# Reordering the routing tail of a mixture-of-experts kernel: the last group's gates and one-hot ahead of the lead's norms, free first weights, more constants, norms ahead of transposes

## The chip, the core and the metric

The kernel runs on one core of one Trainium2 chip. The metric is the device time of one execution in microseconds. The core has a matrix engine (PE, with its weight loads as PEld), a vector engine (DVE), an activation engine (ACT), GpSimd (POOL) and a queue engine (SP) that issues most DMAs. The engines run side by side and wait for each other through semaphores.

## The reference

```python
kv = np.einsum('bhsd,bhse->bhde', k, v)            # 8 batches, 8 heads, 576 tokens, 64 wide
out = np.einsum('bhsd,bhde->bhse', q, kv)
rms = np.sqrt(np.mean(out * out, axis=-1, keepdims=True) + 1e-06)
x = (out / rms * g_norm)                           # then 4608 rows of 512
...
logits = x @ w_gate
e_idx = np.argmax(logits, axis=1)                  # one expert of 8 for each row
probs = np.exp(logits - logits.max(-1, keepdims=True))
probs /= probs.sum(-1, keepdims=True) + 1e-09
eom = 1.0 / (1.0 + np.exp(-(x @ w_output_gate)))
for e in range(E):
    h = np.maximum(x[mask] @ w1[e], 0.0)           # 512 -> 1024
    out[mask] = gate_w[mask, None] * eom[mask, e, None] * (h @ w2[e])
```

## The kernel before, in words

The 4608 rows are 36 tiles of 128. A first stage makes kv for each batch, then the attention rows of each tile (`out_tile`, L779), their squares (L795, summed on DVE at L805) and the gate products. Rows go to a scratch tensor `xs` in DRAM, because the second stage reads them sorted by expert.

**Routing.** The tiles form three groups of 16, 10 and 10 (`GR`). `route(gi)` is a generator of ten steps: 1 the norms (L826 to L842), 2 the gate products scaled by them (`gp`, L850), 3 the logits' sum, maximum and one-hot (`lg` to `ohb`, L854 to L873), 4 the ranks' matmuls (`mrp<-erow`, `ohsum`, `ohb`, L886 to L893) and the output gate (L899 to L902), 5 two exponentials on ACT (L905, L906), 6 slots and scales (L909 to L926) and the rows' write to `xs` (`xwrite`, L980), 7 the row patterns `rrl` and `la` (L933 to L940, `la` partly on POOL), 8 ten or sixteen small matmuls and the lead expert's index (L943 to L952), 9 the patterns `rrc` for all experts (L956 to L959), 10 their matmuls (L962).

**The lead.** The expert with most rows among the first 16 tiles is known early. Its first 256 rows are the lead: `gather(0)` (L250, an indirect DMA on POOL from `xs`) fetches two tiles `xg`; `stage(0, k)` scales each by its norms on DVE (`scale_heads`, L268), copies a column (`tl`, L287), transposes on PE (`tps`, L291) and copies to `xT` on ACT (L294). Eight `lead1` (L320, `hps`) are the first weight product, sixteen matmuls at L567 (`yps`) the second.

**The second run.** The rest of the same expert's rows, 436, come with `gather(1)` in four tiles. `stage(1, k)` stands behind the lead's last matmuls f = 4 to 7 of L567: norms on DVE (L268), `tl`, four transposes on PE, a copy to `xT` on ACT (L299) and its remainder on DVE (L300). Its first product (`mm1`, L341) needs all four tiles. Runs 2 to 8, one expert each, follow on PE.

**What sets the order.** On PE, ACT, DVE and POOL the instructions stand as the program writes them. SP's order is set by a scheduler. After the last tile the string `TAIL` gives the order by hand: `Q` finishes the rows, a digit advances that group's `route`, `W` loads the lead's second weights, `C` issues eight matmuls on constants (L687, `kvp<-ones`) whose result nobody reads, `L` is the next step of the lead (two stages, eight `lead1`), `g` is `gather(1)`, `K` ranks the other experts.

**DMA order.** Rows of the first 16 tiles are written once all inputs are loaded; then the lead's four first-weight loads (`wraw`, 512 KB each, L197) are issued, with `behind` making them wait for a row write, and then the rows of group 1:

```python
for c in range(4):
    behind(wload(0, 1, c), written[0 if c > 1 else -1])
open_rows(1)
```

DMAs on SP use eight semaphores in turn (DMAHW0 to DMAHW7); a DMA waits until the one before it on the same semaphore has landed.

Of the kernel before, what the change touches and what calls it, by code (L numbers as in the profile page):

```python
# [42 lines left out]
TMAX = 6  # L43
# [11 lines left out]
RUNS = [(0, 0, LEAD), (0, LEAD // P, CAP[0] - LEAD)] + [(p, 0, CAP[p]) for p in range(1, E)]  # L55
# [16 lines left out]
PLACES = ['P', 'P', 'VVP']  # L72

HOOKS = {34: "G"}
TAIL = "Q1W2CCCCCCLL122LL22L22LL2gL00L11L22K"

COLD = (24, (8, 8, 10, 5), 5, 4, 12, 8)

# [45 lines left out]
def tiles_of(i):  # L124

    _, t0, n = RUNS[i]
    return [(t0 + k, k * P, min(P, n - k * P)) for k in range(-(-n // P))]
# [6 lines left out]
def body(ctx: ExitStack, tc: tile.TileContext, kvm, rem, qT, wg, gn, w1, w2, kc, xs, tab, out):  # L134
    nc = tc.nc
# [35 lines left out]
    def take(shape, dt, name):  # L171

        i = (rfree if name == "xrow" else free).pop(0)
        t = mem.tile(shape, dt, name=name, tag=f"slot{i}")
        held[id(t)] = (i, t)
        return t

    def give(t):
        i, t = held.pop(id(t))
        (rfree if loads and i >= SLOTS - ROWS else free).append(i)  # L180
# [3 lines left out]
    def expert(p, eng):  # L184
        e = ET.Pool if eng is nc.gpsimd else ET.SP
        k = (p, eng is nc.gpsimd)
        if k not in ereg:
            ereg[k] = nc.values_load(epos[0:1, p:p + 1], engines=(e,), min_val=0, max_val=E - 1)
        return ereg[k]
# [3 lines left out]
    def wload(p, which, c, eng=None):  # L193
        r = take([P, 1024], F32, "wraw")
        eng = eng or nc.sync
        src = (w1 if which == 1 else w2)[ds(expert(p, eng), 1), c]
        d = eng.dma_start(out=r, in_=src.rearrange("o p x -> p (o x)"))  # L197
        raw[(p, which, c)] = r
        return d
# [35 lines left out]
    xg, tails, xT, hT = {}, {}, {}, {}  # L235
# [3 lines left out]
    def behind(a, b):  # L239

        tc.add_manual_dep(a.ins, b.ins.name,
                          mybir.DependencyInfo(mybir.DependencyClass.Sync, mybir.DependencyReason.DATA),
                          reason="place in time")
# [21 lines left out]
    def scale_heads(x, eng):  # L265
        v = x[:, 0:DM].rearrange("p (h d) -> p h d", d=D)
        f = x[:, C_RMS:C_RMS + H].unsqueeze(2).to_broadcast([x.shape[0], H, D])
        return eng.tensor_tensor(out=v, in0=v, in1=f, op=ALU.mult)  # L268

    def scale_rows(i, k0=0, k1=TMAX, after=None):  # L270
        for k, (t, c0, M) in list(enumerate(tiles_of(i)))[k0:k1]:
            scaled = scale_heads(xg[(RUNS[i][0], t)][:M], nc.gpsimd)
            if after is not None:
                behind(scaled, latest[after])

    def stage(i, k):
        p = RUNS[i][0]
        t, c0, M = tiles_of(i)[k]
        x = xg.pop((p, t))
        scale_heads(x[:M], nc.vector)  # L280
        if k == 0:
            if i == 0:
                xT[i] = take([P, 4, LEAD], F32, "xT")
            else:
                xT[i] = [[mem.tile([P, 4, CMAX], F32R, name="xT", tag=f"xT{j}")] for j in range(2)]
        tl = cst.tile([P, 1], F32, name="tl", bufs=14)
        nc.vector.tensor_copy(tl[:M], x[:M, C_SCALE:C_SCALE + 1])  # L287
        tails[(p, t)] = tl
        ps = ps_b.tile([P, 2, 512], F32, name="tps", tag="big")[:, 0].rearrange("p (c m) -> p c m", c=4)
        for c in range(4):  # L290
            nc.tensor.transpose(ps[:, c, :M], x[:M, c * P:(c + 1) * P], ident[:M, :M])  # L291
        give(x)
        if i == 0:
            nc.scalar.activation(xT[0][:, :, c0:c0 + M], ps[:, :, :M], AF.Copy, scale=gcol[:, 0:1])  # L294
            return
        for j, (hi, lo) in enumerate(zip(*xT[i])):
            n = hi.shape[1]
            v = ps[:, j * n:(j + 1) * n, :M]
            nc.scalar.copy(hi[:, :, c0:c0 + M], v)  # L299
            nc.vector.tensor_tensor(out=lo[:, :, c0:c0 + M], in0=v,  # L300
                                    in1=hi.bitcast(F32)[:, :, c0:c0 + M], op=ALU.subtract)
# [357 lines left out]
    for i in range(2):  # L659
        o = c1.tile([P, GMAX + 1, E], BF16, name=f"ohb{i}")  # L660
# [82 lines left out]
    while g < NT:  # L743
        if g == 0:
            k = NT - sum(BIG.values()) - 2 * ROWS
            x = c1.tile([P, k, XW], F32, name="xrow0")
        elif g in BIG:
            k = BIG[g]
            x = mem.tile([P, k, XW], F32, name="xrow", tag=f"xT{list(BIG).index(g)}")
        else:  # L750
            k = 2
            x = take([P, k, XW], F32, "xrow")
# [5 lines left out]
    def out_tile(g):  # L758
        gi, t, n = group_of(g)
        if t == 0:  # L760
            gst[gi] = (sm.tile([P, GMAX, E], F32, name="ss"),
                       sm.tile([P, max(GR[gi % 2::2]), 16, H], F32, name=f"gp{gi % 2}", bufs=1),
                       sm.tile([P, GMAX, 16], F32, name="lg"))
        ps = ps_b.tile([P, 2, 512], F32, name="ops", tag="big")
        parts = []
        n0 = g * P
        while n0 < (g + 1) * P:
            b = n0 // S
            n1 = min((g + 1) * P, (b + 1) * S)
            parts.append((b, n0 - g * P, n1 - n0))  # L770
            n0 = n1
        v = ps[:, :, 0:NP * W].rearrange("q u (p y) -> q u p y", p=NP)
        for p in range(NP):
            for b, r0, m in parts:
                q0 = g % 2 * P + r0

                for u in range(2):
                    r = slice(u * D, (u + 1) * D)
                    nc.tensor.matmul(v[r0:r0 + m, u, p, :], qt[g // 2][r, p, q0:q0 + m], augs[b % 3][r, p, :],  # L779
                                     start=True, stop=True)  # L780
        if g % 2:
            give(qt.pop(g // 2))
        outs.append((g, ps))

    def out_rows():

        g, ps = outs.pop(0)
        gi, t, n = group_of(g)
        ss, gp, lg = gst[gi]
        c0, k, x = next(c for c in chunks if c[0] <= g < c[0] + c[1])  # L790
        xrow = x[:, g - c0]
        v = ps[:, :, 0:NP * W].rearrange("q u (p y) -> q u p y", p=NP)
        nc.scalar.copy(xrow[:, 0:DM].rearrange("q (p u d) -> q u p d", p=NP, u=2), v[:, :, :, 0:D])
        sq = wk.tile([P, H, D], F32, name="sq", bufs=3)
        nc.scalar.activation(sq.rearrange("q (u p) d -> q u p d", u=2), v[:, :, :, 0:D], AF.Square)  # L795
        nc.scalar.copy(gp[:, t].rearrange("q x (u p) -> q u p x", u=2), v[:, :, :, D:W])
        squares.append((sq, ss[:, t, :], gi if t + 1 == n else None))
# [169 lines left out]
            vec.tensor_tensor(out=tsum, in0=tps, in1=tsum, op=ALU.add)  # L967

    xwrites = []
    written = []  # L970
    lead_known = []

    opened = [False, False]
# [1 line left out]
    def xwrite(g, o, i):  # L975
        late = g >= LEAD_TILES
        if not opened[late]:
            xwrites.append((g, o, i))
            return
        written.append(nc.sync.dma_start(out=o, in_=i))  # L980
        if id(i) in held:
            give(i)

# [14 lines left out]
    def steps(at):  # L998
        for gi in list(routing):
            for _ in range(STEPS[gi].get(at, 0)):  # L1000
                advance(gi)

    def run_out(limit):
        nonlocal done_tiles
        if done_tiles < limit:
            out_tile(done_tiles)
            done_tiles += 1
            if len(outs) > 1:
                out_rows()
            if len(squares) > 1:  # L1010
                sums()
            steps(done_tiles)
            load()
            if not loads and not opened[0]:
                open_rows(0)
            if lead_known and opened[0] and not opened[1]:
                for c in range(4):
                    behind(wload(0, 1, c), written[0 if c > 1 else -1])
                open_rows(1)
            for step in HOOKS.get(done_tiles, ""):  # L1020
                act(step)
# [25 lines left out]
    def p1_main():  # L1047
# [16 lines left out]
        while done_tiles < NT:  # L1064
            run_out(NT)
        for step in TAIL:
            act(step)
# [134 lines left out]
    with fixed:  # L1202
# [12 lines left out]
        for i in range(len(RUNS)):  # L1215
# [57 lines left out]
            def put(k, f, e, *a):  # L1273
                at.setdefault(k, {}).setdefault(f, []).append(lambda: e(*a))
# [4 lines left out]
            end = order[T - 1]  # L1279
            if i == 0:  # L1280
                for k in range(len(tiles_of(1))):
                    put(end, 4 + k, stage, 1, k)
            if i > 1:
                put(order[0], 0, begin, i, 1)
# [4 lines left out]
            if change:  # L1289
# [11 lines left out]
                for j in range(2):  # L1301
                    k = 3 + j + (i == 1)
# [20 lines left out]
    with ExitStack() as p3:  # L1323
# [4 lines left out]
        with tc.For_i(0, nreg) as i:  # L1328
# [19 lines left out]
            for w in (w1, w2):  # L1348
                for c in range(4):
                    t = wo.tile([P, 1024], F32, name=f"ow{len(ws)}")  # L1350
                    nc.sync.dma_start(out=t, in_=w[ds(eo, 1), c].rearrange("o p x -> p (o x)"))
                    ws.append(t)
            x = so.tile([P, XW], F32, name="ox")
# [9 lines left out]
            for f in range(8):  # L1363
                ph = pt.tile([P, P], F32, name="oph")
                for d in range(4):
                    o = d * 256 + (f % 2) * P
# [3 lines left out]
            for f in range(8):  # L1370
# [5 lines left out]
                                         in_=y, in_offset=None, bounds_check=NTOK - 1, oob_is_err=False)  # L1376
# [49 lines left out]
```

## Time and profile before

| what | value |
|---|---|
| median of three runs | 567.3 us (566.47 to 567.6) |
| the profiled execution's own time | 567.28 us |
| its span in the trace | 565.4 us |
| PE busy, weight loads | 538.2 us (95%), 460.1 us (81%) |
| DVE, ACT, POOL busy | 386.5 us (68%), 295.1 us (52%), 265.8 us (47%) |
| DMA | 92.28 MB, mean 163 GB/s |
| mean granted clock of PE | 0.985 |

The span runs from the first to the last instruction; 1.9 us of the execution lie around it. PE is nearly always busy, so the stretches in which it is not, or in which its clock is granted at half, carry most of what can be changed by order alone.

### The profile page before, as it was taken

To read this page: it belongs to the slowest core of one execution; us is meant where nothing else is said; L and a number is where in the kernel's file an instruction comes from. 1 tells how busy PE (TensorE), PEld (TensorE's weight loads), DVE (VectorE), ACT (ScalarE), POOL (GpSimd) and SP (SyncE) were. 2 spreads that over 40 slices of the span, in tenths; PEclk is the share of its full clock that TensorE was granted. 3 is DMA by queue.
4 is the path that set the end of the run, shared out by engine and by line. 5 is a ranking of instruction groups with operands and counts; after the bars stand their busy time and mean duration, and the time that the engine had idled before them with its cause. 6 is when DMAs were issued, how large, how long until landed. Compare 5 with 4: busy or idle time off the path is not lost.

```text
span 565.4 us, 11013 instructions
## 1 busy us (share of the span) xinstructions
PE 538.2 (95%) x4104; PEld 460.1 (81%) x4104; DVE 386.5 (68%) x820; ACT 295.1 (52%) x604; POOL 265.8 (47%) x295
## 2 busy tenths in 40 slices
PE   9999994997999999999999999999999999999995
PEld 6888883853978997889889878987898789779974
DVE  2236994673579978847994898577757978896700
ACT  1577881222456746545564456555554656475510
POOL 3001255131498168414970595079408943991021
PEclk9999997799999999999999999999999999999998
DMA  7999998851403360425125513450525054215001
GB/s 302 417 416 416 415 368 308 330 191 56 168 24 112 134 204 22 152 92 174 69 86 172 160 61 112 147 197 20 187 70 192 35 188 129 107 51 175 2 23 44
DMA packets 28424, 92.28 MB, mean 163 GB/s; under 512 B 3825, under 2 KB 3825, under 8 KB 28368
## 3 DMA queue, kind: packets, MB, share of 16 engines
q1 hardware_dynamic: 21936, 71.63, 34.7%
q0 software_dynamic: 6432, 19.92, 10.3%
q8 instruction: 34, 0.56, 0.4%
q14 instruction: 22, 0.18, 0.1%
HBM read 72.34 MB, written 19.70 MB: 163 GB/s over the span
## 4 chain that ended last, share of the span: by engine, by line
PE 62%; DVE 14%; DMA 7%; issue 6%; POOL 5%; ACT 4%; SPq 1%; POOLq 0%; ACTq 0%; DVEq 0%
PE yps L586 25%; PE hpsa L474 13%; PE hpsd L474 6%; PE hps L474 4%; DMA xg<-xs,gidx 3%; PE yps L580 3%; PE hps L320 3%; DVE hT L497 3%; DVE ss L805 2%; PE ops L779 2%; DMA ld<-qT 2%; DMA ld<-kvm 2%; POOL xg L268 2%; PE kvp L704 2%; ACT hT L494 2%
## 5 line engine op out<-in xcount | busy, mean ns | idle before, releaser
L586 PE MATMUL yps<-whi,hT 128*128 128x512 f32 (+3 forms) x560 | 185.0, 396 | 0.5 <-DVE hT L497 0.4
L586 PEld LDWEIGHTS yps<-whi,hT 128*128 128x128 f32 (+3 forms) x560 | 103.9, 186 | 24.1 <-DVE hT L497 1.3
L586 PE MATMUL yps<-wlo,hT 128*128 128x512 f32 (+3 forms) x280 | 109.9, 392 | 0.0
L600 POOL DMA_INDIRECT out<-y,oidx x42 | 51.0, 1213 | 124.9 <-ACT y L599 79.2
L250 POOL DMA_INDIRECT xg<-xs,gidx x42 | 44.9, 1070 | 88.4 <-ACT hT L494 28.1
L497 DVE SCALAR_TENSOR_TENSOR hT<-ct,hT 128x256 fp32r<-128x256 f32 (+6 forms) x88 | 52.2, 623 | 22.6 <-ACT hT L494 22.6
L586 PEld LDWEIGHTS yps<-wlo,hT 128*128 128x128 f32 (+3 forms) x280 | 52.1, 186 | 9.9
L494 ACT ACTIVATE hT<-ct 128x328 fp32r<-128x328 f32 (+13 forms) x56 | 34.4, 614 | 43.0 <-DVE ct L508 43.0
L474 PE MATMUL hpsd<-xT,wh 128*128 128x328 f32 (+6 forms) x224 | 48.3, 302 | 1.7 <-DVE ct L541 1.7
L474 PE MATMUL hpsa<-xb,wh 128*128 128x328 f32 (+6 forms) x224 | 48.2, 303 | 1.1 <-ACT sn L540 0.7
L474 PE MATMUL hpsa<-xT,wh 128*128 128x328 f32 (+6 forms) x224 | 47.5, 300 | 0.0
L268 POOL TENSOR_TENSOR xg<-xg 128x512 f32<-128x512 f32 (+7 forms) x36 | 42.3, 1184 | 9.8 <-DVE ct L529 9.5
L805 DVE TENSOR_REDUCE ss<-sq 128x8 f32<-128x512 f32 x36 | 23.8, 680 | 30.1 <-ACT sq L795 30.1
L399 DVE SCALAR_TENSOR_TENSOR wl<-wraw,gcol,wh 128x512 fp32r<-128x512 f32 (+1 forms) x56 | 43.8, 821 | 0.2 <-ACT wh L398 0.2
L227 DVE TENSOR_TENSOR wlo<-wraw,whi 128x1024 fp32r<-128x1024 f32 x32 | 39.9, 1247 | 5.7 <-ACT whi L224 5.5
L599 ACT ACTIVATE y<-yps,tl 128x512 f32<-128x512 f32 (+3 forms) x37 | 25.5, 689 | 33.3 <-PE yps L586 19.2
L474 PEld LDWEIGHTS hpsd<-xT,wh 128*128 128x128 f32 x224 | 36.6, 188 | 5.1 <-DVE ct L541 3.9
L474 PEld LDWEIGHTS hpsa<-xb,wh 128*128 128x128 f32 x224 | 36.6, 188 | 4.9 <-ACT sn L540 4.2
L399 DVE SCALAR_TENSOR_TENSOR wl<-ws,gcol,wh 128x1024 fp32r<-128x1024 f32 x28 | 40.0, 1429 | 0.0
L779 PE MATMUL ops<-aug,ld 64*128 64x80 f32 (+1 forms) x640 | 39.3, 271 | 0.3 <-issue 0.2
L474 PEld LDWEIGHTS hpsa<-xT,wh 128*128 128x128 f32 x224 | 37.0, 188 | 1.7 <-ACT sn L532 0.3
L779 PEld LDWEIGHTS ops<-aug,ld 64*128 64x128 f32 (+1 forms) x640 | 33.8, 176 | 3.6 <-issue 1.6
(233 smaller groups left out, 1156.8 us busy)
## 6 DMA issues: line engine op xcount, KB each, us to landing
wraw<-w SPq DMA_DIRECT2D x64, 512.0 KB, 4.4
ld<-kvm SPq DMA_DIRECT2D x32, 512.0 KB, 9.9
ld<-qT SPq DMA_DIRECT2D x18, 512.0 KB, 10.0
xs<-xrow SPq DMA_DIRECT2D x9, 528.0 KB, 11.4
xs<-xrow SPq DMA_DIRECT2D x2, 1320.0 KB, 7.4
xs<-xrow SPq DMA_DIRECT2D x1, 2112.0 KB, 12.4
ld<-rem SPq DMA_DIRECT2D x4, 512.0 KB, 9.9
xg<-xs,gidx POOLq DMA_INDIRECT x42, 4.0
```

The costliest lines, as they stand in the source:

```text
L227: eng.tensor_tensor(out=lo, in0=r, in1=hi.bitcast(F32), op=ALU.subtract)
L250: gathered = nc.gpsimd.indirect_dma_start(out=x[:M, :], out_offset=None, in_=rows, in_offset=bass.IndirectOffsetOnAxis(ap=gidx[:M, p, t:t ...
L268: return eng.tensor_tensor(out=v, in0=v, in1=f, op=ALU.mult)
L399: nc.vector.scalar_tensor_tensor(out=lo, in0=x, scalar=gcol[:, 0:1], in1=hi.bitcast(F32), op0=ALU.mult, op1=ALU.subtract)
L474: nc.tensor.matmul(ps, W[a][d], X[b][d], start=start and k == 0, stop=k == 5, skip_group_check=not start)
L494: S.activation(hh, x, AF.Relu)
L497: V.scalar_tensor_tensor(out=v(o, j1 - j0), in0=x[..., j0:j1], scalar=0.0, in1=hh[..., j0:j1].bitcast(F32), op0=ALU.max, op1=ALU.subtract)
L586: nc.tensor.matmul(ps[:M], a, b, start=(f == 0 and j == 0), stop=(f == 7 and j == 2))
L599: nc.scalar.activation(y[:M], ps[:M], AF.Copy, scale=tl[:M, 0:1])
L600: i_ = nc.gpsimd.indirect_dma_start(out=out, out_offset=bass.IndirectOffsetOnAxis(ap=oidx[:M, p, t:t + 1], axis=0), in_=y[:M], in_offset=N ...
L779: nc.tensor.matmul(v[r0:r0 + m, u, p, :], qt[g // 2][r, p, q0:q0 + m], augs[b % 3][r, p, :], start=True, stop=True)
L805: nc.vector.tensor_reduce(out=o, in_=sq, axis=AX.X, op=ALU.add)
```

## The change

```diff
-TAIL = "Q1W2CCCCCCLL122LL22L22LL2gL00L11L22K"
+TAIL = "Q1W2CCCCCCCCCCC22LL22LL22LL12gLL00L11L22K"
...
-    def scale_rows(i, k0=0, k1=TMAX, after=None):
+    def scale_rows(i, k0=0, k1=TMAX, after=None, eng=nc.gpsimd):
         for k, (t, c0, M) in list(enumerate(tiles_of(i)))[k0:k1]:
-            scaled = scale_heads(xg[(RUNS[i][0], t)][:M], nc.gpsimd)
+            scaled = scale_heads(xg[(RUNS[i][0], t)][:M], eng)
...
         x = xg.pop((p, t))
-        scale_heads(x[:M], nc.vector)
+        if i == 0:
+            scale_heads(x[:M], nc.vector)
...
-    written = []
...
-        written.append(nc.sync.dma_start(out=o, in_=i))
+        nc.sync.dma_start(out=o, in_=i)
...
                 for c in range(4):
-                    behind(wload(0, 1, c), written[0 if c > 1 else -1])
+                    wload(0, 1, c)
                 open_rows(1)
...
             if i == 0:
                 for k in range(len(tiles_of(1))):
+                    put(end, k, scale_rows, 1, k, k + 1, None, nc.vector)
                     put(end, 4 + k, stage, 1, k)
```

The string has 11 `C` for 6, so 88 constant matmuls for 48. Group 2's steps 2 and 3 stand ahead of the lead's two stages, its steps 4 and 5 ahead of the first `lead1`, its steps 6 and 7 ahead of the third; step 8 of groups 1 and 2 and `gather(1)` stand behind the fourth, and two `lead1` instead of one stand between `gather(1)` and group 0's step 9.

DVE behind group 2's norms (`rv` in the row above these): `xg` and `tl` are the lead's two stages, `tsl` is group 1's step 8, the others group 2's steps 2 to 4. Before:

```order
L268 TENSOR_TENSOR xg<-xg 128x512
L287 COPY tl<-xg 128x1
L268 TENSOR_TENSOR xg<-xg 128x512
L287 COPY tl<-xg 128x1
L947 TENSOR_TENSOR tsl<-mrp,tsl 128x12
L850 TENSOR_TENSOR gp_1195<-gp_1195,rv 128x10x64 x2
L854 TENSOR_REDUCE lg<-gp_1195 128x10x8
L861 TENSOR_REDUCE mx<-lg 128x10
```

After:

```order
L851 TENSOR_TENSOR gp_1195<-gp_1195,rv 128x10x64 x2
L855 TENSOR_REDUCE lg<-gp_1195 128x10x8
L862 TENSOR_REDUCE mx<-lg 128x10
L864 TENSOR_TENSOR rd<-lg,mx 128x80
L867 SCALAR_TENSOR_TENSOR rsc<-rd,cf 128x80
L869 TENSOR_REDUCE rsx<-rsc 128x10
L873 MEMSET ohb_121 128x4
L874 TENSOR_TENSOR ohb_121<-rsc,rsx 128x80
L268 TENSOR_TENSOR xg<-xg 128x512
L288 COPY tl<-xg 128x1
L268 TENSOR_TENSOR xg<-xg 128x512
L288 COPY tl<-xg 128x1
```

The gates and the one-hot moved ahead of the lead's norms, and `tsl` moved far behind them.

SP behind the last of the five lead row writes; `xs<-xrow` are group 1's row writes, `wraw<-w` the lead's first weights, and the brackets name what each waits for. Before:

```order
L980 DMA xs<-xrow 128x2x528 [waits DVE_49,DMAHW3_49,Activation_49,Pool_49]
L197 ISA
L197 DMA wraw<-w 128x1024 [waits DMAHW4_49,DMAHW2_49,PE_49]
L197 ISA
L197 DMA wraw<-w 128x1024 [waits DMAHW5_49,PE_49]
L197 ISA
L197 DMA wraw<-w 128x1024 [waits DMAHW6_49,PE_49]
L197 ISA
L197 DMA wraw<-w 128x1024 [waits DMAHW7_49,PE_49]
L980 DMA xs<-xrow 128x2x528 [waits DVE_49,DMAHW0_49,Activation_49,Pool_49]
```

After:

```order
L197 DMA wraw<-w 128x1024 [waits DMAHW3_49,PE_49]
L197 ISA
L197 DMA wraw<-w 128x1024 [waits DMAHW4_49,PE_49]
L197 ISA
L197 DMA wraw<-w 128x1024 [waits DMAHW5_49,PE_49]
L197 ISA
L197 DMA wraw<-w 128x1024 [waits DMAHW6_49,PE_49]
L980 DMA xs<-xrow 128x2x528 [waits DVE_49,DMAHW7_49,Activation_49,Pool_49]
L980 DMA xs<-xrow 128x2x528 [waits DVE_49,DMAHW0_49,Activation_49,Pool_49]
```

The weights stand ahead of all of group 1's row writes now, and the wait for the last lead row write (DMAHW2) is gone from the first of them; DMAHW6 of the fourth is the first lead row write.

DVE at the second run, behind the split of two weights; `xg` are the norms, `xT` the remainders. Before:

```order
L268 TENSOR_TENSOR xg<-xg 128x512
L287 COPY tl<-xg 128x1
L300 TENSOR_TENSOR xT<-tps,xT 128x4x128
L268 TENSOR_TENSOR xg<-xg 128x512
L287 COPY tl<-xg 128x1
L300 TENSOR_TENSOR xT<-tps,xT 128x4x128
```

After:

```order
L268 TENSOR_TENSOR xg<-xg 128x512 x3
L268 TENSOR_TENSOR xg<-xg 52x512
L288 COPY tl<-xg 128x1
L301 TENSOR_TENSOR xT<-tps,xT 128x4x128
L288 COPY tl<-xg 128x1
L301 TENSOR_TENSOR xT<-tps,xT 128x4x128
```

All four norms stand ahead of the first remainder now.

## Rows read from the trace of the kernel before

**Rows 1.** The page's first part: busy us, share, instructions.
```profile
PE 538.2 (95%) x4104; PEld 460.1 (81%) x4104; DVE 386.5 (68%) x820; ACT 295.1 (52%) x604; POOL 265.8 (47%) x295
```

**Rows 2.** Windows of 2.5 us: length, busy of PE, PEld, DVE, ACT, POOL, granted clock, DMA share, GB/s.
```profile
90.00:92.50 2.50, 0.00 (x0) 0.00 (x0) 0.11 (x1) 0.00 (x0) 2.46 (x5) 0.78 0.96 361
...
102.50:105.00 2.50, 2.50 (x8) 1.96 (x7) 2.08 (x8) 0.38 (x1) 0.00 (x0) 0.50 1.04 392
105.00:107.50 2.50, 2.50 (x24) 2.17 (x23) 0.79 (x5) 0.64 (x3) 0.00 (x0) 0.99 0.77 313
```

**Rows 3.** PE in order of time: start, length, instruction, count, idle before it.
```profile
83.73 5.08 PE L687 MATMUL kvp<-ones 128*128 128x256 bf16 x45
96.63 1.08 PE L291 MATMUL tps<-ident,xg 128*128 128x128 f32 x4 [7.82 <-DVE tl L287]
98.15 1.08 PE L291 MATMUL tps<-ident,xg 128*128 128x128 f32 x4 [0.43 <-DVE tl L287]
...
100.01 6.20 PE L320 MATMUL hps<-xT,wraw 128*128 128x256 f32 x16 [0.53 <-ACT xT L294]
106.05 0.20 PE L886 MATMUL mrp<-erow,row 128*128 128x88 bf16 x1
...
106.44 5.41 PE L320 MATMUL hps<-xT,wraw 128*128 128x256 f32 x24
...
114.67 0.84 PE L962 MATMUL mrp<-rrc,la 128*128 128x96 bf16 x16 [0.74 <-DVE rrc L959]
...
119.99 11.39 PE L567 MATMUL yps<-wraw,hT 128*128 128x512 f32 x26
131.22 0.60 PE L291 MATMUL tps<-ident,xg 128*128 128x128 f32 x4
131.65 1.02 PE L567 MATMUL yps<-wraw,hT 128*128 128x512 f32 x2
133.92 0.66 PE L291 MATMUL tps<-ident,xg 128*128 128x128 f32 x4 [1.24 <-DVE tl L287]
...
139.26 0.42 PE L291 MATMUL tps<-ident,xg 52*128 52x52 f32 x4 [1.18 <-issue]
140.10 0.88 PE L341 MATMUL hps<-xT,whi 128*128 128x436 f32 x2 [0.42 <-ACT xT L299]
```

**Rows 4.** DVE in order of time.
```profile
89.87 0.24 DVE L840 SCALAR_TENSOR_TENSOR rv<-ru,ry 128x80 f32<-128x80 f32 x1
95.68 0.69 DVE L268 TENSOR_TENSOR xg<-xg 128x512 f32<-128x512 f32 x1 [5.57 <-DMA xg<-xs,gidx]
...
97.20 0.69 DVE L268 TENSOR_TENSOR xg<-xg 128x512 f32<-128x512 f32 x1 [0.77 <-DMA xg<-xs,gidx]
...
99.61 1.55 DVE L850 TENSOR_TENSOR gp<-gp,rv 128x640 f32<-128x640 f32 x2
...
103.18 0.81 DVE L854 TENSOR_REDUCE lg<-gp 128x80 f32<-128x640 f32 x1
...
126.56 0.68 DVE L268 TENSOR_TENSOR xg<-xg 128x512 f32<-128x512 f32 x1
```

**Rows 5.** SP's DMA issues in order of time.
```profile
86.88 2.13 SPq L197 DMA_DIRECT2D wraw<-w  x4
```

**Rows 6.** POOL's gathers in order of time.
```profile
89.21 0.96 POOL L250 DMA_INDIRECT xg<-xs,gidx  x1 [0.30 <-DVE ry L837]
...
118.59 1.04 POOL L250 DMA_INDIRECT xg<-xs,gidx  x1 [8.97 <-DVE tsum L967]
```

**Rows 7.** DMA issues of 89.0 to 89.5, median us from issue to landing.
```profile
xg<-xs,gidx POOLq DMA_INDIRECT x1, 8.0
```

**Rows 8.** The same of 118.4 to 119.0.
```profile
xg<-xs,gidx POOLq DMA_INDIRECT x1, 3.5
```

**Rows 9.** Two windows, columns as in rows 2.
```profile
83.00:87.00 4.00, 4.00 (x43) 3.56 (x40) 3.90 (x19) 2.67 (x7) 0.00 (x0) 1.00 0.42 151
...
87.00:88.00 1.00, 1.00 (x12) 0.89 (x10) 0.90 (x6) 0.00 (x0) 0.18 (x1) 1.00 1.03 389
```

## The prediction

> **What bounds the kernel now.** The page's first part comes first: PE is busy for 95% of the span [rows 1], so only the stretches where it is idle, or granted half its clock, have time to give. The windows of 2.5 us show where that is: PE does nothing from 90 to 92.5, its granted clock is 0.78 there on average, 0.50 still from 102.5 to 105, and 0.99 from 105 on [rows 2]. The order of time on PE gives the waits one by one [rows 3]. The constants begin at 83.73 and last 5.08 us, to 88.8. Then PE waits 7.82 us for the lead's first scaled tile. It transposes two tiles, waits 0.53 for their copy, and starts the lead's first product at 100.01 at half clock. At 114.67 it waits 0.74 for group 0's patterns. Between the lead's last matmuls and the second run's four transposes stand three waits of 1.24 (shown), a like one, and 1.18 us. The order of time on DVE tells who is late [rows 4]. The lead's two norms wait for the gather (until 95.68 and 97.20), while DVE has been idle since `rv` at 90.1; group 2's gates begin only behind them, at 99.61. At the second run each norm stands behind the remainder of the tile before it, so each transpose waits for a copy on ACT, a remainder and a norm, although the first norm of the four runs at 126.56, 4.7 us ahead of its transpose.
>
> From 140.10 on PE has other work in every window, and what follows is started by PE's progress. So I count what the change does to the start of the second run's first product, 140.10 [rows 3], and let the rest shift by as much.
>
> **The change, part by part.**
>
> *Norms ahead of transposes.* All four norms run in a row from 126.56, at 0.68 us each: done by 129.3, ahead of the first transpose at 131.22 [rows 3, 4]. The three waits go: 1.24 + 1.18 + one between them, taken as their mean of 1.21, makes 3.6 us. A pair on L567 that is followed by a wait takes 1.02 us; the 13 pairs in a row take 11.39 / 13 = 0.88 [rows 3]. Three of those save 0.14 each, 0.4. What is late next is ACT's copy of the last tile (0.42, already there), and that stays. Sum **-4.0 us**. The cover is the 1.9 us between 129.3 and 131.22; if DVE came that much later the first transpose would wait. The rest of the change moves DVE and PE ahead together, and the second gather is moved ahead by more: its rows are written some 7 us earlier, because group 2's ranks, at 106.05 before, come right behind the lead's transposes, at about 98.6. Bounds: 0 (the norms are late all the same) and -4.4 (the last wait gone as well).
>
> *Gates and one-hot ahead of the norms.* From `rv` at 90.1 the two products (1.55) and the sum to one-hot take until 93.7, as they took from 99.61 to 103.18 before [rows 4]. That fits ahead of the gather at 95.68: they cost nothing while the gather lands after 93.7, and if it landed at its earliest, 92.7 (below), up to 1.0. The ranks' matmuls (106.05 to 106.44, 0.39) then fall into the 0.53 us in which PE waits for ACT's copy: -0.39. Group 1's ten small matmuls, which ran in that gap, now stand between two `lead1`: at most the same 0.39 back. With two `lead1` instead of one behind the indices, group 0's patterns have twice the time, and the 0.74 us wait at 114.67 goes. Sum **-0.7 us**. Bounds: -1.1 and 0.
>
> *First weights not held back.* The four loads were issued from 86.88, when the last lead row write had landed [rows 5]. Now nothing holds the first three, and the fourth waits only for the first lead row write. They follow the lead's rows in SP's queue and fill engines that run empty from 83 to 87: there the DMA share is 0.42, against 1.03 from 87 to 88 at 389 GB/s [rows 9]. That hole takes (1 - 0.42) x 4 us x 389 GB/s = 0.9 MB of the 2.1 MB. On the other hand group 1's five row writes (528 KB each) are no longer behind the weights' wait. Before, one was issued ahead of the weights and four behind; now all five can be sent as soon as their scales are ready, ahead of the gathers. So the gathers have less of the weights beside them and more rows. The second gather was issued at 89.21 and took 8.0 us beside the weights; with nothing beside it a gather took 3.5 [rows 6 to 8]. So it lands between 92.7 and, if it has to wait for everything in front of it, some 100.4: ahead of it stand 1.2 MB of weights and 2.7 MB of rows instead of 2.1 MB and 0.54 MB, 1.26 MB more, at 389 GB/s 3.2 us. I take 7.0 us, near the loaded end, since the queue is still full: landing at 96.2 instead of 97.2, **-1.0 us**.
>
> The Trainium skill (DMA: Bandwidth & Descriptors, Queues, rings and completion order) says that each DMA engine takes turns between queues, a packet at a time, so a gather on POOL's queue would not stand behind what SP has queued. By that the rows in front cost little and the sum would be nearer the early end. The 8.0 us beside SP's loads [rows 7] is more than turn-taking alone seems to ask for, so the trace agrees with it in part at most.
>
> *More constants.* 40 more at 5.08 / 45 to 5.12 / 48, about 0.107 us, are 4.3 us: PE is busy until 93.1 instead of 88.8. Nothing waits for PE before the first tile's transposes, some 0.95 us behind its gather (96.63 - 95.68), so at 95 or so they cost nothing; with the gather at its earliest, 0.8 at most. What they can bring is the clock. It fell from 1.00 in the window of 90 to 92.5, within 3.7 us of the last constant, and came back about 105, after 5 us of unbroken products [rows 2, 3]. What half clock costs: the first 16 recorded matmuls of `lead1` took 6.20, at full clock 24 take 5.41, so 16 take 3.6; and the second tile's transposes took 1.08 against 0.60 to 0.66. Together 2.6 + 0.4 = 3.0 us. With the constants ending at 93.1, PE still has only two groups of transposes (at most 1.08 each) and 0.39 us of ranks until the product begins at about 98.6 to 99.0: some 5.5 us with 1.3 to 2.5 us of work. Before, the clock fell within 3.7 us of silence. I take it that it falls again and comes back after as long: **0**. Bounds: 0 and -3.0.
>
> *Sum.* -4.0 - 0.7 - 1.0 = -5.7 us, against the profiled execution's 567.28, which is the median (567.3) within 0.02: **561.5 us**. What the second run's later stages need (the second gather, the other experts' ranks, the weight loads behind them) starts earlier by the same or more, so nothing there should give it back.
>
> **The rivals.**
>
> *The clock holds.* The first idle stretch is now about 2 us instead of 7.82, and from 132 to 140 three waits of more than 1 us each between transposes did not lower it [rows 2, 3]. Against it: most of the 5.5 us is idle. Then 3.0 more: 558.5.
>
> *The gather is served in turns.* With the weights out of its way it takes 3.5 to 5 us and lands at 92.7 to 94.2, 3 to 4.5 ahead; less 1.0 for gates and constants that are in its way then, 2.0 to 3.5. That gives 558.5 to 560, and as the idle stretch shrinks with it, the clock may hold too: about 557. For it speaks the hole in the transfers [rows 9], against it the five row writes.
>
> *The gather is served in order.* The row writes in front of it cost the 3.2 us above, and it lands at 100.4: 567.28 + 3.2 - 4.7 = 565.8. For it: 8.0 us beside 2.6 MB is about what that data needs.
>
> *The norms are ahead to no avail.* DVE or the second gather comes too late, and the four transposes wait as before: 561.5 + 4.0 = 565.5. Against it the 1.9 us of cover.
>
> *Slower.* The weights do not use the hole, because the engines that are empty are not those with the long queues, and the gather stands behind all of them, the five row writes and a first load of the second weights: 2.1 + 2.7 + 0.5 MB and the gathers' own 0.54 are 5.86 MB, at 389 GB/s 15.1 us from 87, and 2.8 for a landing (3.5 less its own transfer). It lands at 104.9, 7.7 late, PE idles through it at half clock, and the time is 567.28 + 7.7 - 4.7 = 570.3. It decides from 4.7 us on (landing at 101.9) and is a slowdown beyond 0.2%, 1.13 us, from 103.0. Against it: loads issued 10 us before the gather.
>
> **How the numbers follow.** 0.2% is 1.1 us, about what a measurement of this kernel can tell from no change. The forecast, with the gather some 2 us to either side (559.5 to 563.5), has 0.50; the clock holds 0.23; turns 0.08; in order 0.09; norms to no avail 0.03; a gather so late that it cancels the gain 0.03; slower 0.04. The first five are faster: 0.93. Same 0.03, slower 0.04. The range leaves out the upper rivals and half of the turns, 0.2 or a little more: 557.0 to 564.6.
>
> **What the changed profile would show.** Right: no wait over 0.2 us on PE between the transposes of the second run, whose `mm1` starts 4.7 to 4.9 us after the first of them instead of 8.9; DVE's `gp` from 90.1; no wait ahead of group 0's L962 matmuls; weights issued by SP before 82; the second lead norm at 95 to 98; a clock that dips between 94 and 106. Wrong: a second lead norm beyond 99 or before 94, a clock of 1.00 throughout, or a new wait behind 140 that takes back what came before.

## The result, and the profile after

| what | before | changed |
|---|---|---|
| median, runs of one session | 566.88 us (566.15 to 567.6, 4 runs) | 560.26 us (559.43 to 561.48, 4 runs) |
| the profiled execution's own time, span | 567.28, 565.4 us | 559.43, 557.6 us |
| mean granted clock of PE | 0.985 | 0.994 |

The ratio is 0.9885, with a 95% interval of 0.9861 to 0.9909: the changed kernel is about 6.6 us faster, where 5.8 (561.5 against 567.3) was forecast. The profiled execution was the shortest of the four, so sizes read from it lie on the high side. Line numbers of the changed kernel are one higher than those of before from L288 to the matmuls at L963, and the same again at L980; in e5 and e7 they are one higher still.

PE in order of time, with start, length, instruction, count and the idle time before it, answers to [rows 3]:

```profile
83.22 9.78 PE L688 MATMUL kvp<-ones 128*128 128x256 bf16 x88
95.07 0.63 PE L292 MATMUL tps<-ident,xg 128*128 128x128 f32 x4 [2.07 <-DVE tl L288]
96.67 0.81 PE L292 MATMUL tps<-ident,xg 128*128 128x128 f32 x4 [0.97 <-ACT xT L295]
...
98.25 8.22 PE L321 MATMUL hps<-xT,wraw 128*128 128x256 f32 x32 [0.15 <-ACT xT L295]
106.30 0.40 PE L944 MATMUL mrp<-rrl,la 128*128 128x12 bf16 x10
106.96 0.39 PE L944 MATMUL mrp<-rrl,la 128*128 128x12 bf16 x10 [0.26 <-DVE tsl L948]
107.21 3.70 PE L321 MATMUL hps<-xT,wraw 128*128 128x256 f32 x16
110.75 0.84 PE L963 MATMUL mrp<-rrc,la 128*128 128x96 bf16 x16
...
116.08 11.39 PE L568 MATMUL yps<-wraw,hT 128*128 128x512 f32 x26
127.30 0.60 PE L292 MATMUL tps<-ident,xg 128*128 128x128 f32 x4
...
132.16 0.88 PE L342 MATMUL hps<-xT,whi 128*128 128x436 f32 x2 [0.42 <-ACT xT L300]
```

The constants now take 9.78 us; before, the whole of them began at 83.39 and took 5.41 (48 matmuls), since the first row of [rows 3] starts inside them. The second run's first product begins at 132.16, before at 140.10 [rows 3]: 7.94 us sooner, and the execution is 7.85 us shorter, so nothing behind that point gave the gain back. The 7.94 can be split at three instructions that both traces have.

- From the first transpose of the second run to that product: 4.86 us (127.30 to 132.16) instead of 8.88. That is **-4.02**; the three waits are gone, and only ACT's copy of 0.42 is left. (The third wait of before, which the prediction took as 1.21, was 1.14.)
- To the second lead norm, by DVE's rows below: 95.72 instead of 97.20, **-1.48**. From there to the lead's product 2.53 instead of 2.81, **-0.28**; the second tile's transposes take 0.81 instead of 1.08, because the clock falls later.
- From the lead's product (98.25) to the second product (116.08): 17.83 instead of 19.98, **-2.15**. The wait of 0.74 at L963 is gone. The ranks' 0.39 left this stretch, and group 1's small matmuls came in with 0.65 (106.30 to 107.21 holds both groups' ten, 0.91, where before one group's ten took 0.26, from 111.69 to 111.95). That makes -0.48; what remains, -1.67, is in the main the product running less at half clock.

DVE in order of time, for [rows 4]:

```profile
89.98 0.27 DVE L841 SCALAR_TENSOR_TENSOR rv<-ru,ry 128x80 f32<-128x80 f32 x1
90.35 1.73 DVE L851 TENSOR_TENSOR gp<-gp,rv 128x640 f32<-128x640 f32 x2
...
93.97 0.24 DVE L874 TENSOR_TENSOR ohb<-rsc,rsx 128x80 bf16<-128x80 f32 x1
94.13 0.68 DVE L268 TENSOR_TENSOR xg<-xg 128x512 f32<-128x512 f32 x1
...
95.72 0.69 DVE L268 TENSOR_TENSOR xg<-xg 128x512 f32<-128x512 f32 x1 [0.85 <-DMA xg<-xs,gidx]
...
122.97 2.48 DVE L268 TENSOR_TENSOR xg<-xg 128x512 f32<-128x512 f32 x4
```

Group 2's gates and one-hot fill the time from 90.35 to 94.1. The first lead norm stands right behind them, without a wait; the second waits 0.85 for its gather, at 95.72. POOL issued the two gathers at 87.37 and 88.77:

```profile
87.37 1.09 POOL L250 DMA_INDIRECT xg<-xs,gidx  x1 [9.23 <-DVE rrl L934]
88.77 0.96 POOL L250 DMA_INDIRECT xg<-xs,gidx  x1 [0.30 <-issue]
```

The four norms of the second run end at 125.4, 1.9 us ahead of the transposes at 127.30: the cover that the prediction counted.

Windows of the changed kernel, columns as in [rows 2] and [rows 9]:

```profile
83.00:87.00 4.00, 4.00 (x41) 3.52 (x40) 3.90 (x19) 2.67 (x7) 0.00 (x0) 1.00 1.03 405
...
95.00:97.50 2.50, 1.46 (x12) 1.22 (x13) 1.72 (x4) 0.69 (x1) 2.50 (x5) 0.90 1.05 395
97.50:100.00 2.50, 2.35 (x17) 1.93 (x15) 2.14 (x15) 0.94 (x3) 0.99 (x4) 0.50 1.03 416
100.00:102.50 2.50, 2.50 (x12) 2.15 (x12) 1.71 (x9) 0.38 (x1) 1.11 (x2) 0.92 1.02 403
```

The hole in the transfers from 83 to 87 is filled: DMA share 1.03 where it was 0.42 [rows 9]. The clock is at half in the whole window of 97.5 to 100 and in parts of the two beside it, from about 97.0 to 100.4 by windows of 0.5 us; before it was at half until 105 [rows 2].

SP's issues, for [rows 5]:

```profile
77.48 3.73 SPq L197 DMA_DIRECT2D wraw<-w  x4
85.70 4.24 SPq L980 DMA_DIRECT2D xs<-xrow  x5
```

The four weight loads start at 77.48 instead of 86.88. Group 1's five row writes now go out from 85.70 to 89.9, around the two gathers.

### The profile page after: what moved, and what is told of

Its sections match the earlier page's. It is cut to its first block, busy times and chain, and to the rows that moved or that the text cites. A ratio compares the mean times of both kernels' runs of the same rounds, so it can differ in the third digit from the quotient of the medians.

```text
span 557.6 us, 11092 instructions
## 1 busy us (share of the span) xinstructions
PE 539.2 (97%) x4144; PEld 462.6 (83%) x4144; DVE 387.0 (69%) x820; ACT 295.1 (53%) x604; POOL 268.0 (48%) x295
## 4 chain that ended last, share of the span: by engine, by line
PE 69%; POOL 7%; DMA 7%; DVE 6%; issue 6%; ACT 4%; SPq 1%; POOLq 0%; ACTq 0%
PE yps L587 26%; PE hpsa L475 13%; PE hpsd L475 6%; PE ops L780 5%; PE hps L475 4%; PE kvp L705 3%; PE yps L581 3%; PE hps L321 3%; PE yps L568 2%; DVE hT L498 2%; DMA ld<-qT 2%; DMA ld<-kvm 2%; POOL xg L250 2%; POOL xg L268 2%; DMA wraw<-w 1%
## 5 line engine op out<-in xcount | busy, mean ns | idle before, releaser
L601 POOL DMA_INDIRECT out<-y,oidx x42 | 52.2, 1242 | 122.3 <-ACT y L600 81.9
```

Of the source, the lines that this page charges most:

```text
L601: i_ = nc.gpsimd.indirect_dma_start(out=out, out_offset=bass.IndirectOffsetOnAxis(ap=oidx[:M, p, t:t + 1], axis=0), in_=y[:M], in_offset=N ...
```

## The experiments

Two sessions, four kernels each; the kernel before ran beside them with medians of 566.80 (11 runs) and 567.11 us (11 runs). Ratios compare each kernel with the one before in its own session.

**The changed kernel again (e0).** No edit.

> The changed kernel once more, as the measure for the runs beside it. If the clock's fall between the constants and the lead's first product is what spreads its times, they spread again over some 2 us around 560.3 (559.4 to 561.5), and this profile shows the fall at another place than 97.0 to 100.4, with the second run's first product later by about half of any further time at half clock.

Measured: 560.71 us (560.29 to 562.08, 4 runs), ratio 0.9889 [0.9874, 0.9903]. The profile fell on the longest of the four runs:

```profile
97.42 1.08 PE L292 MATMUL tps<-ident,xg 128*128 128x128 f32 x4 [1.30 <-DVE xg L268]
...
99.28 9.48 PE L321 MATMUL hps<-xT,wraw 128*128 128x256 f32 x32 [0.15 <-ACT xT L295]
...
129.89 0.60 PE L292 MATMUL tps<-ident,xg 128*128 128x128 f32 x4
...
134.75 0.88 PE L342 MATMUL hps<-xT,whi 128*128 128x436 f32 x2 [0.42 <-ACT xT L300]
```

The same program takes 9.48 us for the first 32 recorded matmuls of the lead's first product, where the first profile had 8.22, and its second norm stands at 96.47 instead of 95.72. The norms' part is the same 4.86 us. The clock falls at nearly the same place as in the first profile, about 97.2, and not at another as expected, but it comes back only at about 104.0 instead of 100.4. So one program differs from run to run by some 2 us, through the length of the stretch at half clock and the landing of one gather.

**The norms alone (e1).** The kernel before, with this part of the change only:

```diff
+                    put(end, k, scale_rows, 1, k, k + 1, None, nc.vector)
                     put(end, 4 + k, stage, 1, k)
...
-        scale_heads(x[:M], nc.vector)
+        if i == 0:
+            scale_heads(x[:M], nc.vector)
```

> The kernel before with one part of the change: the second run's four norms ahead of its transposes. Theory (three waits of 1.2 us on PE go, and nothing later takes it back): 4.0 us faster than before, 566.9 to 562.9, the first product 4.9 us behind the first transpose instead of 8.9. Rival (DVE or the gather is late all the same, or a later stage waits instead): no change or less than 2 us.

Measured: 563.25 us (562.60 to 563.68, 5 runs), ratio 0.9933 [0.9920, 0.9946], 3.8 us of 567. Its transposes and the product behind them:

```profile
131.15 0.60 PE L292 MATMUL tps<-ident,xg 128*128 128x128 f32 x4
...
136.01 0.88 PE L342 MATMUL hps<-xT,whi 128*128 128x436 f32 x2 [0.42 <-ACT xT L300]
```

They are again 4.86 us apart, and all that stands ahead of them is as before (the second product at 119.93, before 119.99). This part is worth its nearly 4 us by itself, and leaves some 2.5 for the rest.

**The first weights held back (e2).** The changed kernel, with the old wait put back:

```diff
-                    wload(0, 1, c)
+                    behind(wload(0, 1, c), written[0 if c > 1 else -1])
```

> The changed kernel with the first weights held behind the row writes again. Theory (the weights beside the gather are what makes it slow): the second lead tile is scaled at about 97.2 instead of 95.7, and with a longer idle stretch behind the constants the clock is low for longer: 1.5 to 3 us slower than the changed kernel, 561.8 to 563.3. Rival (group 1's rows, which now stand in front of the gather, slow it as much as the weights did): landing at 95.7 or earlier, 560.3 or less.

Measured: 562.01 us (560.08 to 564.18, 6 runs), ratio 0.9918 [0.9899, 0.9938], against 0.9889 for the change. The weights are issued at 85.91 again, but the second norm starts between the two profiles of the changed kernel (95.72 and 96.47):

```profile
95.94 0.69 DVE L268 TENSOR_TENSOR xg<-xg 128x512 f32<-128x512 f32 x1 [0.66 <-DMA xg<-xs,gidx]
```

So the time is in the theory's range, but the profile does not show the later landing (97.2) that was to cause it; the medians differ by 1.3 us with overlapping intervals. Whether the free weights bring something by themselves stays open.

**Six constants (e3).** The changed kernel with the old number of `C`:

```diff
-TAIL = "Q1W2CCCCCCCCCCC22LL22LL22LL12gLL00L11L22K"
+TAIL = "Q1W2CCCCCC22LL22LL22LL12gLL00L11L22K"
```

> The changed kernel with six groups of constants instead of eleven. Theory (the constants shorten the time at half clock and do nothing else): the gather lands as in the changed kernel, the clock falls before the first transposes and rises later, so the lead's first matmuls run longer at half clock: 1 to 2.6 us slower, 561.3 to 562.9. Rival (the clock falls and rises the same way whatever the constants do): 560.3, and the low stretch as long as with eleven.

Measured: 560.97 us (560.86 to 562.71, 5 runs), ratio 0.9903 [0.9889, 0.9917]: 0.3 us more than the changed kernel by medians, 0.8 by ratios, inside the intervals. Three of its windows show why so little:

```profile
92.50:95.00 2.50, 0.00 (x0) 0.00 (x0) 1.15 (x6) 0.00 (x0) 2.50 (x5) 0.50 1.03 397
...
100.00:102.50 2.50, 2.50 (x8) 2.11 (x9) 2.36 (x17) 0.04 (x1) 1.62 (x3) 0.69 0.87 349
102.50:105.00 2.50, 2.50 (x13) 2.21 (x12) 0.82 (x5) 0.77 (x2) 0.20 (x1) 1.00 1.01 381
```

The clock is at half earlier, in the whole window of 92.5 to 95, but PE does nothing there; the product's first 32 matmuls, from 99.83, take 8.02 us, no more than the 8.22 and 9.48 with eleven. By windows of 0.5 us the clock is low from about 91.3 to 101.6; with eleven groups it fell at 97.0 and 97.2 and came back at 100.4 and 104.0. So constants that end before the next work put the fall off, but no gain of theirs shows in the product or in the time. Neither expectation came out: the low stretch is longer, as the theory had it, but the product is not.

**One more constant in the gap (e4).** The changed kernel with 13 `C`, and one `C` between the lead's two stages:

```diff
-TAIL = "Q1W2CCCCCCCCCCC22LL22LL22LL12gLL00L11L22K"
+TAIL = "Q1W2CCCCCCCCCCCCC22LCL22LL22LL12gLL00L11L22K"
```

> The changed kernel with 13 groups of constants ahead of the gates and one more between the lead's two transposes, so that PE idles for 1.5 us and less at a time. Theory (what is left of the clock's cost is set by idle time between the constants and the product): the clock stays at 1.00 through the tail, the product runs at full rate from its first matmul, 1.3 to 2.8 us faster than the changed kernel, 558 to 559.4. Rival (the clock falls at whatever idle stretch there is, and the constants only delay the transposes): 560.3 or slower, with the clock at half for 3 us or more.

Measured: 559.41 us (558.56 to 559.79, 4 runs), ratio 0.9869 [0.9854, 0.9883]. All windows from 90 to 105 have a granted clock of 1.00, and so have those up to 117; the lead's first product runs at full clock throughout:

```profile
94.86 0.63 PE L292 MATMUL tps<-ident,xg 128*128 128x128 f32 x4 [0.29 <-DVE tl L288]
95.32 1.04 PE L688 MATMUL kvp<-ones 128*128 128x256 bf16 x8
97.36 0.63 PE L292 MATMUL tps<-ident,xg 128*128 128x128 f32 x4 [1.01 <-DVE xg L268]
...
98.77 7.17 PE L321 MATMUL hps<-xT,wraw 128*128 128x256 f32 x32 [0.39 <-ACT xT L295]
```

7.17 us is what the 32 matmuls take at full clock. By that measure the changed kernel lost 1.05 us in its first profile (8.22) and 2.31 in its second (9.48). The gain of 1.1 us by ratios (0.0020 of 567) is of that size, though the two intervals overlap a little. The mean granted clock is plainer: 0.997 or 0.998 in all four executions, 0.991 to 0.995 in the eight of the changed kernel. The edit adds constants in two places, ahead of the gates and in the gap; which of them keeps the clock up was not run apart.

**Group 1's rows behind the second gather (e5).** The changed kernel, with the five row writes made to wait for the lead's second gather:

```diff
             xg[(p, t)] = x
+            latest['gather'] = gathered
...
-        nc.sync.dma_start(out=o, in_=i)
+        d = nc.sync.dma_start(out=o, in_=i)
+        if LEAD_TILES <= g < sum(GR[:2]):
+            behind(d, latest['gather'])
```

> The changed kernel with group 1's row writes held until the second lead gather has landed, so the gather has next to nothing beside it. Theory (whatever SP has queued in front of the gather slows it): the gather takes 3.5 to 5 us instead of 7, the second lead tile is scaled at 93 to 94 instead of 95.7 to 96.5, and the time falls by about 2 us, to 558.5; the rows land later but the second run's gather still lands ahead of its norms. Rival 1 (the queues take turns, and the rows in front do not matter): landing as in the changed kernel, 560.5. Rival 2 (the held rows push the last group's rows and with them the second run's gather past 125): slower, 561 to 564.

Measured: 558.72 us (558.02 to 558.92, 4 runs), ratio 0.9852 [0.9837, 0.9866], 2.1 us less than the changed kernel (0.0037 of 567). POOL's second gather, and DVE in order of time:

```profile
89.19 0.96 POOL L250 DMA_INDIRECT xg<-xs,gidx  x1 [0.30 <-issue]
...
93.96 0.24 DVE L875 TENSOR_TENSOR ohb<-rsc,rsx 128x80 bf16<-128x80 f32 x1
94.12 0.70 DVE L269 TENSOR_TENSOR xg<-xg 128x512 f32<-128x512 f32 x1
...
94.81 0.71 DVE L269 TENSOR_TENSOR xg<-xg 128x512 f32<-128x512 f32 x1
```

And SP's issues:

```profile
93.06 4.37 SPq L981 DMA_DIRECT2D xs<-xrow  x5
```

The rows leave at 93.06, when the second gather, issued at 89.19, has landed: at most 3.9 us, against 6.95 in the changed kernel (88.77 to 95.72) and 7.74 in its second profile (88.73 to 96.47). Both norms now run without a wait; it is the one-hot that they stand behind, which is why the second is scaled at 94.81 and not at the theory's 93 to 94. The packets show where the 3 us were. Packets, MB and share of 16 engines by queue, q1 for SP's and q0 for POOL's transfers; the changed kernel from 89 to 91, and below the dots from 91 to 93:

```profile
q1 hardware_dynamic: 367, 0.80, 103.7%
...
q1 hardware_dynamic: 273, 0.54, 73.7%
q0 software_dynamic: 61, 0.24, 30.0%
```

And e5 in the same two windows:

```profile
q0 software_dynamic: 65, 0.22, 42.9%
q1 hardware_dynamic: 83, 0.29, 36.1%
...
q0 software_dynamic: 95, 0.32, 49.5%
q1 hardware_dynamic: 3, 0.00, 0.6%
```

In the changed kernel no packet of a gather moves from 89 to 91, although the first was issued at 87.37; from 91 on the two queues share the engines. In e5 65 packets of the gathers move in these two microseconds. DVE's gates, which run beside the gathers in both, are not needed for this: the kernel before, whose DVE was idle from 90.1, moved none from 89 to 91 either, beside these packets of SP's:

```profile
q1 hardware_dynamic: 187, 0.69, 97.0%
```

So what SP has queued costs the gather twice: its first packets come some 2 us later, and then it has part of the engines only. The second weights stand behind the rows on SP and are held with them (97.67, in the changed kernel 90.18), so the rows' share is not taken apart from theirs.

Not all of the 2.1 us is the gather. The lead's product starts at 97.43, which is 0.8 us earlier than in the changed kernel's first profile (98.25) and 1.85 earlier than in its second (99.28). The clock adds to it: the product's first 32 matmuls take 8.13, near the 8.22 of the first profile, and all four executions have a mean granted clock of 0.994 or 0.995, while three of the changed kernel's eight have 0.991 or 0.992.

The price of holding them back is cover: the second run's gather goes from 112.24 to 117.34, and its four norms end at 125.6, only 0.8 us ahead of the transposes at 126.40.

**The gates behind the norms (e6).** The changed kernel with the old order of `TAIL` and 11 `C`:

```diff
-TAIL = "Q1W2CCCCCCCCCCC22LL22LL22LL12gLL00L11L22K"
+TAIL = "Q1W2CCCCCCCCCCCLL122LL22L22LL2gL00L11L22K"
```

> The changed kernel with the old order of group 2's steps (gates and one-hot behind the lead's norms), but with eleven groups of constants, free weights and the norms ahead of the transposes. Theory (the order is worth the wait at group 0's patterns and the ranks' matmuls, and no more): the 0.74 us wait ahead of those patterns is back, 0.4 to 1.1 us slower than the changed kernel, 560.9 to 561.6. Rival (the old order starts the last group's rows 7 us later, and the second run's gather comes too late for its norms): the first transpose of the second run waits, 2 us slower or more.

Measured: 562.32 us (559.36 to 563.58, 6 runs), ratio 0.9913 [0.9893, 0.9933], 1.4 us more than the changed kernel by ratios, with overlapping intervals. The forecast's term was 0.7. The two things it named are back in the trace, and the rival is not: no wait stands ahead of the second run's first transpose, at 129.87.

```profile
99.68 5.19 PE L321 MATMUL hps<-xT,wraw 128*128 128x256 f32 x16 [0.53 <-ACT xT L295]
...
113.32 0.84 PE L963 MATMUL mrp<-rrc,la 128*128 128x96 bf16 x16 [0.74 <-DVE rrc L960]
```

The wait of 0.74 at L963, and 0.53 ahead of the lead's product with nothing but group 1's small matmuls in the gap. The rest of the 1.4 is within what the clock and the gather (second norm at 96.87) change from run to run: the one execution with a mean granted clock of 0.994 took 559.36, the five with 0.989 to 0.992 took 562.0 to 563.6.

**Rows behind the gather and constants in the gap (e7).** e5 with 12 `C` and the `C` in the gap:

```diff
+TAIL = "Q1W2CCCCCCCCCCCC22LCL22LL22LL12gLL00L11L22K"
```

> The two suspected costs taken away together: rows held behind the gather, 12 groups of constants and one between the lead's transposes. Theory (both act on their own): the sum of the two single gains, 2 for the gather and 1.3 to 2.8 for the clock, 556 to 557.5. Rival (with the gather early the idle stretch is short anyway, so the constants add nothing): as with the rows alone, 558.5.

Measured: 557.48 us (556.88 to 557.64, 5 runs), ratio 0.9831 [0.9818, 0.9844]: the best of all, 9.6 us below the kernel before and 3.3 below the changed one. That is the sum of what e4 (1.1) and e5 (2.1) gave, at the slow end of the theory's 556 to 557.5:

```profile
95.08 0.63 PE L293 MATMUL tps<-ident,xg 128*128 128x128 f32 x4 [1.46 <-DVE tl L289]
...
97.80 7.17 PE L322 MATMUL hps<-xT,wraw 128*128 128x256 f32 x32 [0.39 <-ACT xT L296]
...
130.66 0.87 PE L343 MATMUL hps<-xT,whi 128*128 128x436 f32 x2 [0.42 <-ACT xT L301]
```

The clock stays at 1.00, and PE's longest wait here, 1.46, is for the norms behind group 2's one-hot on DVE, which run at 94.03 and 94.72 without a wait of their own: what bounds this place now is DVE, no longer a transfer.

## Why the prediction was right, and where its sizes were off

**Norms ahead of transposes, -4.0: right in size and cause.** -4.02 in the trace, 3.8 us when done alone (e1). No wait of 0.2 us or more is left between the transposes, and the 1.9 us of cover held.

**Gates and one-hot, -0.7: right in mechanism, near in size.** By its own rows the part is -0.48 (0.74 and 0.39 gone, 0.65 come in); as what is left of the 7.94 it is -0.6 (less 4.02, 1.48 and the clock's 1.8). Group 1's small matmuls cost more than "at most the same 0.39", because PE waits 0.26 for `tsl` between the two groups. Both mechanisms that were named came back when the order was undone (e6). In time that cost 1.4 with a wide interval, so the runs do not settle the size. The gates were done at 94.1 in the first profile, forecast 93.7, and delay the first lead norm there; in e5 and e7 they delay both. In the second profile of the changed kernel they were done at 93.1, and the first norm waited for its gather until 94.54.

**First weights, -1.0: the sizes -1.48 and -0.73 lie around it, but not for the reason given.** The landing forecast at 96.2 came at 95.7 and 96.5. Of the 1.48 us and 0.73 us gained, 0.44 and 0.48 are an earlier issue of the gather (88.77 and 88.73, before 89.21). The step "I take 7.0 us" is the one that was mis-sized: from its issue to the second norm the gather took 6.95 and 7.74 us, and 8.02, 7.78 and 7.70 in the other profiles with free weights and rows in front (e3, e4, e6). With the weights held it took 7.99 before, 7.90 in e1 and 7.70 in e2. So free weights did not make the gather clearly faster, and that the landing came near the forecast is in part luck. What sets it is what SP has queued beside the gather: with group 1's rows and the second weights held back it took at most 3.9 (e5).

The rival in which the gather is served in turns is refuted as forecast, since it took 6.95 us or more and not 3.5 to 5; its time was also added up wrongly, since 567.28 less 4.7 and less 2.0 to 3.5 is 559.1 to 560.6 and not 558.5 to 560. The one served in order would have been at 100.4 and is refuted too.

The Trainium skill (DMA: Bandwidth & Descriptors, Queues, rings and completion order) has each engine take turns between queues, a packet at a time. From 91 us on the trace agrees in so far as both queues move (30.0% and 73.7% of the engines from 91 to 93), but not from 89 to 91, where SP's queue had all of them while a gather was issued; the measurement decides here. Whether the gather had packets ready in those two microseconds no view shows.

**More constants, 0: a mis-sized term.** The step "I take it that it falls again and comes back after as long" failed in its second half. The clock did fall again in all profiles with eleven constants ahead of the gates, but it came back sooner: in the first profile at about 100.4, while before it was still at half at 105. That was worth 1.8 us there (0.28 + 1.55, the latter from 2.6 - 1.05), and 0.3 in the second profile, where the product lost 2.31. It is not shown that the added constants brought it: with six (e3) the product lost 0.85 by its profile, and the second tile's transposes some 0.4. What decides after how long the clock returns, and why that differs between runs of one program, stays open. No row shows the 5.12 us from which the constants' price was taken; the 40 more took 4.37 us (9.78 less 5.41), near the 4.3 forecast.

With the second profile's sizes the sum is 5.2 us (567.28 to 562.08), near the forecast's 5.7; with the first it is 7.85. The medians, 6.1 and 6.6 below the kernel before, lie between. The signs that the prediction named as right came as well: 4.86 us between the transposes and the product, no wait ahead of L963 in the first profile, weights issued at 77.48, the second lead norm at 95.7 and 96.5, and a clock that dips between 97 and 104. So 4.0 us of the forecast are understood, and the other 1.7 fit because they lie inside what one program varies by (3.8 and 1.2 in the two profiles). Of the rivals none came true: in e4 the clock holds, at 559.41, but this takes more constants, some of them in the gap.

**Attribution.** Undone one at a time, the parts are worth 1.6 (e2), 0.8 (e3) and 1.4 us (e6) by ratios, 3.8 in all, while e1 leaves 2.5 for them. Their intervals are as wide as the differences, and the mean granted clock of each execution shows what most of that width is. The changed kernel's eight executions took 559.4 to 561.0 us where it was 0.994 or 0.995 (five of them) and 560.5 to 562.1 where it was 0.991 or 0.992 (three). e2 took 560.1 at 0.994 (one), 561.1 to 562.9 at 0.991 or 0.992 (four) and 564.2 at 0.988 (one), and e6 goes the same way. So e2 and e6 are slower in the main because more of their executions had a longer stretch at half clock; whether their edits cause that or chance does, six executions of each do not tell. Only the norms' part (e1) and the gain of e5 as a whole are settled in size; that constants in the gap keep the clock up (e4, e7) is settled, their gain of some 1 us less so.

## What to carry to other kernels

When an instruction of one tile stands in a chain through three engines, put the steps that need nothing of the chain ahead of it for all tiles; here the gain, counted link by link from the trace, came out within 0.1 us (4.02 for 4.0). Before a short critical gather, look at what the other queues have been given, and hold back what nobody needs yet: in e5 that gained 2.1 us, and its price was cover further on (0.8 us left of 1.9). Filler matmuls paid here when they reached to the next real work and stood in its gaps (559.4 us); eleven groups that ended before it (560.7) were not clearly worth more than six (561.0). And when a result agrees with a sum, check each term by itself: here one term held, and the others agreed only within the spread of one program.

## What the hardware showed that was not expected

- A gather issued on POOL at 87.37 moved no packet until 91 while SP's queue had 103.7% of the engines' time (89 to 91); from 91 to 93 it had 30.0% of it, beside SP's 73.7%.
- POOL's ten `la` took 7.69 us (from 89.77) beside group 2's gates on DVE; before, with DVE idle from 90.1 on, they took 5.84, and with the gates behind the norms again (e6) 6.02.
- The granted clock came back at different times in runs of one program: the product's first 32 matmuls took 8.22 us in one profile and 9.48 in another, 7.17 where it never fell.
